# The first sequence's sums of y for layer three: asked for at turns 46 to 52 of layer one, and kept in two tiles

## The chip, the cores and the metric

The kernel runs on one core of a Trainium2 chip, as one launch. The metric is the device time of the launch in microseconds, the median over several executions. One more execution was taken with the hardware profiler; every row below comes from it. Engines are named as in the profile: PE is TensorE (matmuls; PEld its weight loads), DVE is VectorE, ACT is ScalarE, POOL is GpSimd, SP is SyncE, whose queue issues the transfers.

## The reference

Two batch entries ("sequences") of 768 tokens, 512 features; all float32.

```python
x = attention(q, k, v)            # 8 heads of 64; local window and block summaries; 1536 tokens x 512
h = max(x @ w1, x @ w2, x @ w3)   # layer one, 768 wide, a maximum over three products
y = h @ w_out                     # layer two, 512 wide
z = (y @ w_a) * (y @ w_b)         # layer three, 1536 wide, a product of two products
out = z @ w_out2                  # layer four, 512 wide
```

## The kernel before

**Tiles.** The 1536 tokens lie in four chunks of 384, two for each sequence: chunks 0 and 1 are the first sequence, 2 and 3 the second. Features lie on the 128 partitions. Each matrix product is made of three float32r matmuls (high by high, low by high, high by low part), by `mm3` (L511), so an operand is kept as a high part, written by ACT, and a low part, the remainder, written by DVE or POOL (`split`, L514 and L515).

**Layers one and two** (`layers12`) run chunk by chunk. A turn of layer one is 12 matmuls into one PSUM tile `ph` (4 blocks of features, 3 matmuls each); `evac` takes the result out into a tile `t`, by ACT for the first of three (L536) and by DVE, with the maximum, for the other two (L538). The third is split into `hg`, by ACT and POOL. Layer two is four products `py` of 18 matmuls each; ACT copies each into `y` (L564). One chunk has 18 + 4 = 22 turns. The list `TURNS[0]` lays the turns of all chunks out in one order: turns 0 to 43 are chunks 0 and 1, turns 44 to 51 are chunk 2 alone, 52 to 71 alternate between chunks 2 and 3, 72 to 75 are layer two of chunk 2, and 76 to 87 are the rest of chunk 3.

**Layer three** (`layer3`) forms y @ w_a and y @ w_b by a scheme with seven products instead of eight, over both chunks of a sequence and both halves of the features. Its moving operands are seven sums (B11, B21, T1, T2, T3, B22, T4) of quarters of y. `sums_of(c, m)` makes them: the tiles `yd` are differences (DVE, L580); `op` then writes each operand `yt` as a high part (ACT, L575) and a low part (DVE, L576). For the second sequence, `halves` calls it as soon as y is there. For the first sequence y is complete after turn 43, and the main loop calls it at the four turns of `SUMS`: B11, then B21, then T1, then T2, T3, B22 and T4 together. The products go to PSUM tiles `qb`, `qg` and `qd`; ACT and DVE take them out (`s`, `m`, `u` by ACT at L621; `ca` at L631; `t` at L635 and L637).

**Weights.** A weight tile `w` (128x512, 64-bit source) is loaded by SP's queue, put together by ACT (L441, L443), DVE (L445, L446) and POOL (L447), and split into `wt` by ACT (L451) and DVE or POOL (L452). For layer three two such tiles are also combined into sums `s` by DVE (L467 to L470) before the split. Layers three and four alternate over six groups of 256 columns; layer four's products are `po`, added up in `acc`.

**What sets the order.** The program text sets only priorities and dependences. A scheduler, when the kernel is built, puts each engine's instructions into one queue; each engine then works its queue strictly in that order, and an instruction that waits holds up all behind it. `tc.issue_after` adds an order between two instructions on one engine. Layer-three products of the first sequence are put by the scheduler between the `ph` and `py` products of chunks 2 and 3, so part of layer three is done while the layers before it still run.

The lines that call the sums:

```python
GATE, ROOM, SUMS, EARLY34 = (2, 3), 16, (58, 62, 66, 70), 6
...
            with tc.issue_after(mark[0]), tc.issue_after(mark[1]):
                weights(1)
                if i in SUMS:
                    m = SUMS.index(i)
                    sums_of(m // 2, m % 2 * 2 + 1)
```

Of the kernel before, what the change touches and what calls it, by code (L numbers as in the profile page):

```python
# [10 lines left out]
F32R = mybir.dt.float32r  # L11
# [8 lines left out]
P = 128  # L20
# [16 lines left out]
NCH, MAXT = len(CHUNKS), max(SIZES)  # L37
# [21 lines left out]

GATE, ROOM, SUMS, EARLY34 = (2, 3), 16, (58, 62, 66, 70), 6
LEAD, TURN, ERA0, ASKS, AHEAD, PRE, TURNS = 5, (11, 2, 2), 8, (3, 4, 5, 7, 9), (4, 1), 3, ((6, N1 - 6, 6, 4, 4, 8, N1 - 8, 4, 12), (24, 34), (34, 44))


# [11 lines left out]
def attention_then_maxout_then_bilinear(ctx: ExitStack, tc: tile.TileContext, qt, kt, vt, vwin, wall, const, out):  # L77
# [13 lines left out]
    t_p = ctx.enter_context(tc.tile_pool(name="t", bufs=B))  # L91
# [465 lines left out]
        if lastc:  # L557
            w_freed += N2

    ops = {}  # L560

    def halves(c, m, ps):

# [4 lines left out]
    def sums_of(c, m):  # L568

        b, j = divmod(c, 2)  # L570
        (b11, b21), (b12, b22) = ((y[:, 0:2], y[:, 2:4]) for y in (ys[2 * b], ys[2 * b + j]))

        def op(name, src):
            ops[b, name] = t = t_p.tile([P, 2, 2, MAXT * P], F32R, tag=name, name="yt")
            A.activation(t[:, 0], src, AF.Copy)  # L575
            V.tensor_tensor(t[:, 1], src, t[:, 0], ALU.subtract)  # L576

        def diff(tag, x, y):
            t = y_p.tile([P, 2, MAXT * P], F32, tag=tag, name="yd")
            V.tensor_tensor(t, x, y, ALU.subtract)  # L580
            return t

        if j == 0:
            op(("B11", "B21")[m // 2], (b11, b21)[m // 2])
        elif m == 1:
            t1 = sums[b] = diff("t1", b12, b11)
            op("T1", t1)
        else:
            t2 = diff("t2", b22, sums[b])
            op("T2", t2)  # L590
            op("T3", diff("t3", b22, b12))
            op("B22", b22)
            op("T4", diff("t3", b21, t2))
# [201 lines left out]
```

## Time and profile before

| | |
|---|---|
| median of 3 runs | 566.62 us (566.19 to 566.95) |
| the profiled execution | 569.36 us, of which the span from first to last instruction is 567.6 us |
| PE busy | 548.9 us, 97% of the span, 3374 matmuls |
| DVE, ACT, POOL busy | 376.3 us (66%), 278.9 us (49%), 203.0 us (36%) |
| mean granted clock of PE | 0.993 of full speed |

PE is busy nearly all the time, so the kernel's time is the matmuls' time plus the pauses of PE and the stretches in which its clock is lowered. In 40 slices of the span the page shows two where the granted clock is 0.9 (near 250 us and near 310 us); the rest from 14 us on is at full speed.

### The profile page before, as it was taken

Reading aid. Unit: us, or ns where it says so; the run is one execution under the profiler, and the core shown is the slowest. Engines: PE = TensorE matmul, PEld = TensorE weight load, DVE = VectorE, ACT = ScalarE, POOL = GpSimd, SP = SyncE. Lnnn points to the kernel's source line nnn. Section 1 sums busy time; section 2 is a strip of 40 time slices with the busy share of each in tenths; the row PEclk is TensorE's granted clock in tenths of the full one; section 3 lists DMA queues with packets and bytes.
Section 4 is the critical chain, followed back from the end, with each engine's and each line's share of the span. In section 5 each row is a group of like instructions: output and inputs, shape, how many; then the busy total and the mean of one; then the engine's idle time right before and its main releaser. Section 6 shows DMA issues by size and latency. Waiting matters only on the chain.

```text
span 567.6 us, 9050 instructions
## 1 busy us (share of the span) xinstructions
PE 548.9 (97%) x3374; PEld 518.4 (91%) x3374; DVE 376.3 (66%) x781; ACT 278.9 (49%) x667; POOL 203.0 (36%) x177
## 2 busy tenths in 40 slices
PE   7999999999999999999998899999999999999997
PEld 7889999999999999999997899899989989999985
DVE  4798966865432133939969955866868997783374
ACT  4799765666441214534656556445454553341220
POOL 3479996442110111503603413413413242330030
PEclk9999999999999999989999899999999999999999
DMA  8992464843100030212231222122123121000005
GB/s 304 354 270 75 151 233 133 252 145 112 46 1 1 2 111 1 75 38 93 93 112 39 74 70 80 38 74 76 37 75 103 46 76 38 1 0 1 1 29 193
DMA packets 16987, 51.81 MB, mean 91 GB/s; under 512 B 2096, under 2 KB 2480, under 8 KB 16944
## 3 DMA queue, kind: packets, MB, share of 16 engines
q1 hardware_dynamic: 16944, 51.25, 27.6%
q8 instruction: 26, 0.43, 0.3%
q14 instruction: 17, 0.14, 0.1%
HBM read 48.09 MB, written 3.15 MB: 90 GB/s over the span
## 4 chain that ended last, share of the span: by engine, by line
PE 67%; DVE 15%; DMA 7%; ACT 5%; issue 2%; POOL 2%; SPq 1%; ACTq 0%; POOLq 0%; DVEq 0%
PE ph L511 21%; PE qb L511 11%; PE py L511 6%; PE qg L511 5%; PE po L666 4%; PE po L667 4%; PE po L668 4%; DMA w<-wall 4%; DVE wt L452 3%; PE ps L250 3%; PE qd L511 2%; PE psv L305 2%; DVE t L637 2%; DVE w L446 2%; DVE hg L515 2%
## 5 line engine op out<-in xcount | busy, mean ns | idle before, releaser
L511 PE MATMUL ph<-x,wt 128*128 128x384 f32 x864 | 156.3, 337 | 0.0
L511 PEld LDWEIGHTS ph<-x,wt 128*128 128x128 f32 x864 | 149.3, 188 | 0.5 <-DVE x L515 0.3
L447 POOL TENSOR_TENSOR w<-w,w 128x512 int32<-128x512 int32 x60 | 83.2, 1391 | 155.1 <-DVE w L446 96.0
L511 PE MATMUL qb<-yt,wt 128*128 128x384 f32 x576 | 114.6, 339 | 5.5 <-DVE t L637 3.0
L511 PEld LDWEIGHTS qb<-yt,wt 128*128 128x128 f32 x576 | 102.6, 189 | 11.1 <-DVE t L637 3.4
L514 ACT ACTIVATE hg<-t 128x384 fp32r<-128x384 f32 x72 | 36.9, 522 | 86.7 <-DVE t L538 47.9
L638 POOL TENSOR_TENSOR t<-t,ca 128x384 f32<-128x384 f32 x36 | 43.8, 1232 | 85.4 <-DVE t L637 85.3
L511 PE MATMUL qg<-yt,wt 128*128 128x384 f32 x288 | 60.0, 345 | 2.0 <-DVE t L637 1.0
L678 DVE TENSOR_TENSOR acc<-po,acc 128x512 f32<-128x512 f32 x60 | 40.8, 686 | 27.1 <-PE po L668 27.1
L538 DVE TENSOR_TENSOR t<-ph,t 128x384 f32<-128x384 f32 x48 | 26.5, 552 | 45.8 <-PE ph L511 44.7
L666 PE MATMUL po<-wt,hg 128*128 128x512 f32 x144 | 56.3, 391 | 0.6 <-ACT hg L514 0.6
L667 PE MATMUL po<-wt,hg 128*128 128x512 f32 x144 | 56.6, 393 | 0.0
L511 PEld LDWEIGHTS qg<-yt,wt 128*128 128x128 f32 x288 | 52.4, 194 | 4.5 <-DVE t L637 1.7
L668 PE MATMUL po<-wt,hg 128*128 128x512 f32 x144 | 56.1, 395 | 0.1
L511 PE MATMUL py<-hg,wt 128*128 128x384 f32 x288 | 56.0, 343 | 0.1
L511 PEld LDWEIGHTS py<-hg,wt 128*128 128x128 f32 x288 | 50.2, 190 | 0.5 <-ACT y L564 0.4
L257 ACT ACTIVATE s<-s,nm 128x120 f32<-128x120 f32 x96 | 37.1, 390 | 23.2 <-DVE nm L256 22.6
L515 POOL TENSOR_TENSOR hg<-t,hg 128x384 fp32r<-128x384 f32 x24 | 27.1, 1134 | 50.5 <-ACT hg L514 49.3
L451 ACT ACTIVATE wt<-w 128x512 fp32r<-128x512 f32 (+1 forms) x60 | 35.1, 586 | 18.6 <-PE qb L511 14.4
L515 DVE TENSOR_TENSOR hg<-t,hg 128x384 fp32r<-128x384 f32 x48 | 40.6, 855 | 3.9 <-ACT hg L514 3.9
L452 DVE TENSOR_TENSOR wt<-w,wt 128x512 fp32r<-128x512 f32 (+1 forms) x44 | 30.5, 694 | 14.4 <-ACT wt L451 14.4
L443 ACT ACTIVATE w<-w 128x512 int32<-128x512 uint32 x60 | 39.2, 667 | 0.6 <-DMA w<-wall 0.6
(80 smaller groups left out, 779.9 us busy)
## 6 DMA issues: line engine op xcount, KB each, us to landing
w<-wall SPq DMA_DIRECT2D x60, 512.0 KB, 3.5
q<-qt SPq DMA_DIRECT2D x15, 384.0 KB, 6.9
row<-kt SPq DMA_DIRECT2D x8, 416.0 KB, 5.0
full<-vt SPq DMA_DIRECT2D x8, 384.0 KB, 7.2
out<-acc SPq DMA_DIRECT2D x12, 256.0 KB, 2.0
v<-vwin SPq DMA_DIRECT2D x12, 192.0 KB, 5.4
v<-vwin SPq DMA_DIRECT2D x12, 96.0 KB, 5.6
q<-qt SPq DMA_DIRECT2D x1, 256.0 KB, 4.1
```

What stands on the lines that cost most here:

```text
L257: A.activation(s[:, a], s[:, a], AF.Exp, bias=nm[:, a:a + 1], scale=-1.0, accum_out=sm[:, a:a + 1])
L443: A.activation(lw.bitcast(I32), lw, AF.Copy, scale=2.0 ** -29)
L447: G.tensor_tensor(w.bitcast(I32), w.bitcast(I32), lw.bitcast(I32), ALU.add)
L452: eng.tensor_tensor(w[:, 1], r, w[:, 0], ALU.subtract)
L511: T.matmul(ps, w[:, i, o:o + P], x[:, j], start=first and n == 0, stop=last and n == 2, skip_group_check=more)
L514: A.activation(dst[:, 0], src, AF.Copy)
L515: eng.tensor_tensor(dst[:, 1], src, dst[:, 0], ALU.subtract)
L638: G.tensor_tensor(t, t, cs[c, f], ALU.mult)
L666: T.matmul(ps, g[:, 0], w[:, 0], start=(f == 0), stop=False)
L667: T.matmul(ps, g[:, 0], w[:, 1], start=False, stop=False)
L668: T.matmul(ps, g[:, 1], w[:, 0], start=False, stop=(f == 1))
L678: V.tensor_tensor(acc[c, i], ps, acc[c, i], ALU.add)
```

## The change

The four turns at which the first sequence's sums are called move from 58, 62, 66 and 70 to 46, 48, 50 and 52. The operands of the first sequence lie in two tiles, one for B11 and B21 and one for T1, T2, T3, B22 and T4, where each had a tile of its own; the second sequence keeps seven tiles.

```diff
-GATE, ROOM, SUMS, EARLY34 = (2, 3), 16, (58, 62, 66, 70), 6
+GATE, ROOM, SUMS, EARLY34 = (2, 3), 16, (46, 48, 50, 52), 6
...
-    ops = {}
+    ops, both = {}, {}
...
         def op(name, src):
-            ops[b, name] = t = t_p.tile([P, 2, 2, MAXT * P], F32R, tag=name, name="yt")
+            names = next(x for x in (("B11", "B21"), ("T1", "T2", "T3", "B22", "T4")) if name in x) if b == 0 else (name,)
+            if name == names[0]:
+                both[b, names] = t_p.tile([P, len(names), 2, 2, MAXT * P], F32R, tag=names[0] + str(b), name="yt", bufs=1)
+            ops[b, name] = t = both[b, names][:, names.index(name)]
             A.activation(t[:, 0], src, AF.Copy)
             V.tensor_tensor(t[:, 1], src, t[:, 0], ALU.subtract)
```

Instructions and their sizes are the same in both kernels; their order differs on every engine's queue. Line numbers behind the new lines are three higher (L576 is L579, L580 is L583). With the two tiles alone, and the old turns, every queue has the order of before.

On DVE, from the first maximum of layer one of chunk 2 on (`t<-ph` are maxima, `yd` and `yt` the sums), the queue before was:

```order
L538 TENSOR_TENSOR t_2333<-ph,t_2318 128x384
L538 TENSOR_TENSOR t_2349<-ph,t_2333 128x384
L538 TENSOR_TENSOR t_2381<-ph,t_2366 128x384
L538 TENSOR_TENSOR t_2397<-ph,t_2381 128x384
L538 TENSOR_TENSOR t_2429<-ph,t_2414 128x384
L538 TENSOR_TENSOR t_2445<-ph,t_2429 128x384
L538 TENSOR_TENSOR t_2493<-ph,t_2463 128x384
L538 TENSOR_TENSOR t_2508<-ph,t_2478 128x384
L538 TENSOR_TENSOR t_2523<-ph,t_2493 128x384
L576 TENSOR_TENSOR yt<-y,yt 128x768
L538 TENSOR_TENSOR t_2544<-ph,t_2508 128x384
L538 TENSOR_TENSOR t_2592<-ph,t_2562 128x384
```

and is now:

```order
L538 TENSOR_TENSOR t_2333<-ph,t_2318 128x384
L579 TENSOR_TENSOR yt<-y,yt 128x768
L538 TENSOR_TENSOR t_2352<-ph,t_2333 128x384
L579 TENSOR_TENSOR yt<-y,yt 128x768
L538 TENSOR_TENSOR t_2386<-ph,t_2369 128x384
L538 TENSOR_TENSOR t_2402<-ph,t_2386 128x384
L583 TENSOR_TENSOR yd<-y 128x768
L579 TENSOR_TENSOR yt<-yd,yt 128x768
L538 TENSOR_TENSOR t_2439<-ph,t_2424 128x384
L583 TENSOR_TENSOR yd<-y,yd 128x768
L583 TENSOR_TENSOR yd<-y 128x768
L579 TENSOR_TENSOR yt<-y,yt 128x768
```

Nearly all sums of the first sequence stand now between the maxima of chunk 2's first eight turns; before, the first of them stood behind nine maxima.

On DVE, where the first three weight tiles of layer three are worked on (`w`, `s`, `wt`) and the last maxima of chunk 2 are taken, the queue before was:

```order
L580 TENSOR_TENSOR yd<-y,yd 128x768
L580 TENSOR_TENSOR yd<-y 128x768
L576 TENSOR_TENSOR yt<-y,yt 128x768
L538 TENSOR_TENSOR t_2785<-ph,t_2711 128x384
L452 TENSOR_TENSOR wt<-w_2722,wt 128x512
L467 TENSOR_TENSOR s<-w_2729 128x256
L469 TENSOR_TENSOR s<-w_2722,w_2729 128x256
L576 TENSOR_TENSOR yt<-yd,yt 128x768 x2
L445 TENSOR_SCALAR w_2897<-psw 128x512
L468 TENSOR_TENSOR s<-s,w_2722 128x256
L452 TENSOR_TENSOR wt<-w_2729,wt 128x256
L580 TENSOR_TENSOR yd<-y,yd 128x768
```

and is now:

```order
L538 TENSOR_TENSOR t_2780<-ph,t_2724 128x384
L452 TENSOR_TENSOR wt<-w_2735,wt 128x512
L467 TENSOR_TENSOR s<-w_2742 128x256
L469 TENSOR_TENSOR s<-w_2735,w_2742 128x256
L468 TENSOR_TENSOR s<-s,w_2735 128x256
L470 TENSOR_TENSOR s<-w_2735,s 128x256
L445 TENSOR_SCALAR w_2892<-psw 128x512
L446 SCALAR_TENSOR_TENSOR w_2892<-psw,w_2892 128x512
L452 TENSOR_TENSOR wt<-w_2742,wt 128x256
L452 TENSOR_TENSOR wt<-s,wt 128x512 x2
L579 TENSOR_TENSOR yt<-y,yt 128x768 x2
```

The sums `yd` and `yt` of the first sequence are gone from between the steps of the weights; the two `yt` at the end are the second sequence's.

On PE, from the end of the last `ph` product before layer two of chunk 2 on, the queue before was:

```order
L511 MATMUL qb<-yt,wt 128x384
L511 MATMUL qd<-yt,wt 128x384
L511 MATMUL py<-hg,wt 128x384 x30
L511 MATMUL qb<-yt,wt 128x384 x5
L511 MATMUL py<-hg,wt 128x384 x4
L511 MATMUL qd<-yt,wt 128x384 x2
L511 MATMUL py<-hg,wt 128x384 x2
L511 MATMUL qd<-yt,wt 128x384 x3
L511 MATMUL qg<-yt,wt 128x384
L511 MATMUL qb<-yt,wt 128x384
L511 MATMUL qg<-yt,wt 128x384 x5
L511 MATMUL qb<-yt,wt 128x384 x5
```

and is now:

```order
L511 MATMUL py<-hg,wt 128x384 x17
L511 MATMUL qb<-yt,wt 128x384 x6
L511 MATMUL py<-hg,wt 128x384 x19
L511 MATMUL qg<-yt,wt 128x384 x6
L511 MATMUL qb<-yt,wt 128x384 x4
L511 MATMUL py<-hg,wt 128x384 x36
L511 MATMUL qb<-yt,wt 128x384 x2
L511 MATMUL qd<-yt,wt 128x384 x3
L511 MATMUL ph<-x,wt 128x384 x12
```

The first layer-three product comes later, behind 17 matmuls of layer two, and six matmuls of it stand together; 25 matmuls stand now between `qb`'s first six and its next four, where 12 stood. From the second sequence's sums on, the queues of all engines have the same order in both kernels, but for a few neighbours on PE (`qg`, `qb`, `po`) and one `yt` on ACT.

## Rows read from the trace of the kernel before

**Rows 1.** Busy time by stretch: PE, PEld, DVE, ACT, POOL, then granted clock, DMA.
```profile
180.00:200.00 20.00, 20.00 (x117) 20.00 (x116) 2.98 (x6) 4.28 (x8) 3.03 (x3) 1.00 0.00 1
...
240.00:260.00 20.00, 18.36 (x95) 17.86 (x94) 10.44 (x17) 6.95 (x13) 3.20 (x3) 0.91 0.08 27
...
280.00:300.00 20.00, 19.14 (x107) 18.17 (x106) 14.53 (x19) 12.29 (x23) 4.21 (x4) 1.00 0.32 103
300.00:320.00 20.00, 16.95 (x88) 16.40 (x87) 19.73 (x30) 10.45 (x22) 10.68 (x8) 0.91 0.13 44
```

**Rows 2.** The same view in stretches of 2 us around both pauses.
```profile
242.00:244.00 2.00, 1.67 (x6) 1.67 (x7) 2.00 (x4) 1.61 (x3) 0.00 (x0) 0.66 0.64 184
244.00:246.00 2.00, 2.00 (x8) 2.00 (x7) 1.08 (x2) 0.80 (x2) 0.00 (x0) 0.50 0.19 78
...
314.00:316.00 2.00, 2.00 (x9) 1.98 (x8) 2.00 (x3) 0.83 (x2) 2.00 (x3) 0.58 0.00 0
316.00:318.00 2.00, 2.00 (x8) 2.00 (x8) 2.00 (x2) 1.01 (x2) 2.00 (x3) 0.56 0.00 0
```

**Rows 3.** Chain that ended last: start, length (us), what; layer-one products without a pause.
```profile
175.24 50.19 PE ph L511 x288
```

**Rows 4.** PE in order of time: start, length (us), tile; idle before and releaser.
```profile
231.50 0.34 PE L511 MATMUL qb<-yt,wt 128*128 128x384 f32 x1
...
240.95 0.44 PE L511 MATMUL qb<-yt,wt 128*128 128x384 f32 x1 [0.71 <-ACT s L621]
242.33 1.72 PE L511 MATMUL qg<-yt,wt 128*128 128x384 f32 x5 [0.94 <-DVE wt L452]
...
255.00 0.34 PE L511 MATMUL qb<-yt,wt 128*128 128x384 f32 x1
...
285.41 6.83 PE L511 MATMUL py<-hg,wt 128*128 128x384 f32 x36
292.07 1.57 PE L511 MATMUL qg<-yt,wt 128*128 128x384 f32 x8
...
299.63 3.41 PE L511 MATMUL qb<-yt,wt 128*128 128x384 f32 x18 [0.73 <-ACT u L621]
...
313.56 1.68 PE L511 MATMUL qb<-yt,wt 128*128 128x384 f32 x6 [3.05 <-DVE t L637]
```

**Rows 5.** DVE in order of time, layer one and the stretch before the first pause.
```profile
210.93 0.56 DVE L538 TENSOR_TENSOR t<-ph,t 128x384 f32<-128x384 f32 x1 [5.70 <-PE ph L511]
...
228.85 1.27 DVE L580 TENSOR_TENSOR yd<-y,yd 128x768 f32<-128x768 f32 x1
230.04 2.06 DVE L580 TENSOR_TENSOR yd<-y 128x768 f32<-128x768 f32 x1
232.03 1.77 DVE L576 TENSOR_TENSOR yt<-y,yt 128x768 fp32r<-128x768 f32 x1
233.73 0.54 DVE L538 TENSOR_TENSOR t<-ph,t 128x384 f32<-128x384 f32 x1
...
235.46 1.81 DVE L576 TENSOR_TENSOR yt<-yd,yt 128x768 fp32r<-128x768 f32 x2
...
238.69 0.95 DVE L580 TENSOR_TENSOR yd<-y,yd 128x768 f32<-128x768 f32 x1
...
240.50 1.78 DVE L452 TENSOR_TENSOR wt<-s,wt 128x512 fp32r<-128x512 f32 x1
```

**Rows 6.** POOL in order of time, the first two weight tiles of layer three.
```profile
228.00 3.29 POOL L447 TENSOR_TENSOR w<-w,w 128x512 int32<-128x512 int32 x2 [8.53 <-issue]
```

**Rows 7.** ACT in order of time, evacuations of the last layer-two products.
```profile
288.31 0.47 ACT L564 ACTIVATE y<-py 128x384 f32<-128x384 f32 x1
...
291.84 0.93 ACT L564 ACTIVATE y<-py 128x384 f32<-128x384 f32 x2
```

**Rows 8.** DVE in order of time, second sequence's sums to second pause.
```profile
292.85 0.95 DVE L580 TENSOR_TENSOR yd<-y,yd 128x768 f32<-128x768 f32 x1
...
312.96 0.54 DVE L637 TENSOR_TENSOR t<-qb,m 128x384 f32<-128x384 f32 x1
```

**Rows 9.** What SP's queue of transfers waited for, 195 to 330 us: total, times, longest.
```profile
SPq L421 <- POOL w L447: 99.4, 12, 18.8
```

## The prediction

> **What bounds the kernel now.** I read the page's busy shares first: PE works 97% of the span at a mean clock of 0.993, so a change that leaves the matmuls alone can gain only what PE loses in pauses and in lowered clock. The forty slices of the page put the lowered clock at two places, and the table of stretches is the view that narrows them down: in the 20 us from 240 and from 300 the granted clock is 0.91, and beside them it is 1.00 [rows 1]. In stretches of 2 us it is 0.66 and 0.50 right behind the first pause, and 0.58 and 0.56 right behind the second [rows 2]; these four account for both 0.91 ((0.34 + 0.50) x 2 / 20 = 0.084, and 0.086), so elsewhere in those 40 us the clock is full. 0.50 is the lower of the clock's two levels, 1.2 GHz against 2.4; the others are mixtures of the two. PE in order of time then shows what each pause waits for [rows 4]: at 240.95 for an ACT copy `s` (0.71 us), at 242.33 for the low part of a weight sum, a `wt` by DVE (0.94), at 299.63 for ACT's `u` (0.73), at 313.56 for DVE's `t` (3.05).
>
> The change rewrites what DVE does ahead of the first pause, so DVE in order of time is the view to stay with [rows 5]. From 228.85 to 242.28 it has no pause; the `wt` that PE waits for ends at 242.28, and PE starts at 242.33. Between 228.85 and that end stand six sums of the first sequence. The rows give `yd` 1.27, `yd` 2.06, `yt` 1.77, two `yt` in 1.81 and `yd` 0.95: 7.86 by durations, about 7.5 from start to next start, since neighbours overlap by some 0.08. So more than half of DVE's 13.4 us there is work that the pause does not need.
>
> **The change, part by part.** It removes no instruction and adds none; it moves them, and the rest is order.
>
> *The sums' new place.* On DVE they go among the first maxima of chunk 2. There DVE is busy 2.98 of 20 us, ACT 4.28 and POOL 3.03 [rows 1], and later it once waits 5.70 us for a product [rows 5]. The eleven steps (four `yd`, seven `yt`) at 0.95 us (the undisturbed row at 238.69) are 10.5 us of DVE work, for which about 17 idle us in every 20 are there. What is queued behind a sum is the next maximum, and behind that the PSUM tile that PE wants again. One product takes 12 x 50.19/288 = 2.09 us [rows 3], of which a maximum uses 0.56 [rows 5], so three sums in a row (0.95 + 0.95 + 0.90 = 2.80) make the next maximum late by 2.80 - 1.53 = 1.27 us. Does PE feel 1.27? The trace of before has such a case: the maximum at 233.73 to 234.27 takes out a product that ended 12 layer-two matmuls (2.09 us) ahead of 231.50, at about 229.4. It came out 4.9 us late, and PE's rows show no wait for it. I cost the new place at nothing, with 4.9 us as cover.
>
> *The first pause (A).* With the sums gone, DVE's chain to the late `wt` is 13.4 - 7.5 = 5.9 us of other rows. What starts that chain is POOL's last step on the first two weight tiles, which ends at 228.00 + 3.29 = 231.29 [rows 6]; 231.3 + 5.9 = 237.2. PE now asks later: 43 matmuls stand between the first product of layer three's old place (231.50 [rows 4]) and the first matmul that needs this `wt` (17 `py`, 6 `qb`, 19 `py` and one), so at 231.5 + 43 x 0.1743 = 239.0. The margin is 1.8 us. The other wait, 0.71 for ACT's `s`, had 12 matmuls (2.1 us) between the product and its reuse, and has 25 (4.4 us) now: 2.1 + 0.71 = 2.8 was needed, 4.4 is there. Both waits should go, and with them the lowered clock. PE from 231.50 to 255.00 [rows 4] spent 23.50 us on 113 matmuls; at 0.1743 each they take 19.70. **A = 3.80 us** (0.71 + 0.94 of waits, 2 x 0.34 + 2 x 0.50 = 1.68 of clock, and 0.47 of smaller gaps). The bounds are 0 (a new wait of the same length) and 3.80.
>
> On that lowered clock, first the rows: at 240.95 to 242.33 PE idled for 1.65 us in two pieces, and 0.66 and 0.50 followed [rows 2, 4]; behind the single pause of 0.73 at 299.63 the clock stayed full, by the account above. The Trainium skill (TensorE: Matmul & The Clock Gate, What's actually happening) says that the gate is set by how busy the engine has recently been, and that the throttled state is the default which activity lifts. Here that agrees with both rows. By it the whole 1.68 comes back with the pauses; were the lowered clock tied to the place in the program and not to idling, the gain would be 3.80 - 1.68 = 2.12.
>
> *The end of layer two (B).* In the last 36 `py` matmuls, 285.41 to 292.07, PE takes 6.66 us for 6.27 of work [rows 4]. Two rows say why: ACT's copy of a `py` tile comes only at 288.31 [rows 7], ACT being held until then behind a weight step that waits for its data. The new order has PE there about 4 us earlier while the weight steps also come earlier, and PE's queue has three other matmul groups ahead of it. **B = 0.39**; bounds 0 and 0.39, or less than nothing if the weight's transfer keeps its old time (a rival, below).
>
> *Start of the second sequence's sums (C).* PE ends the last `py` at 292.07, ACT does two copies in a row from 291.84 (0.93 us) and DVE starts the first `yd` at 292.85, 0.78 later [rows 7, 8]. A single copy takes 0.47, so with the copy of the tile before done in time this is about 0.5: **C = 0.25**; bounds 0 and 0.3.
>
> *The second pause.* From 292.85 to 313.50 DVE works through the second sequence's sums and the weights of the next products, 19.73 busy of the 20 us from 300 [rows 1, 8], and the `t` at the end releases PE at 313.56. This chain is in the same order after, so it keeps its 20.7 us, its start moves with PE, and the waits of 0.73 and 3.05 and the lowered clock behind them stay. Gain 0 here; what was gained ahead is carried through, neither more nor less.
>
> *Transfers.* SP's queue waits, in 195 to 330, 12 times and 99.4 us in all for POOL's `w` step, which frees a weight buffer [rows 9]. So the transfers are paced by the engines, come earlier by what the engines come earlier, and cost nothing; if they were not, the price is in the third rival.
>
> Sum: 3.80 + 0.39 + 0.25 = 4.44 us. The profiled execution's own time is 569.36, so 564.92 by its measure. It lies 2.74 above the median of 566.62; I take the same loss off the median: **562.2**. The forecast's own range is 561.2 to 563.2 (the clock's share moves with where a pause falls; B and C may be nothing).
>
> **The rivals.**
> *Part of the pause stays* (0.10). The wait of 0.71 for `s` is a matter of PSUM tiles and not of DVE. If ACT is again late there, PE idles 0.71, maybe with the lowered clock: 562.2 + 0.71 = 562.9, or with 1.68 of clock 564.6. Against it speak the 25 matmuls of cover. The Trainium skill (Perfetto Trace Analysis, Optimization Strategy) reads a recurring gap as a possible lack of room for the next tile; the 0.71 here, named for ACT's copy out, agrees with that reading, and by it the gap would stay.
>
> *The second pause shrinks too* (0.08). If DVE's freed time lets weight steps run ahead of the second sequence's sums, up to 3.05 of wait and 2 x 0.42 + 2 x 0.44 = 1.72 of clock come back: 562.2 - 4.77 = 557.4, with half of it 559.8. Against it: the queues from there on are in the old order, and a strict order lets nothing slip ahead.
>
> *The gain is given back at the second pause* (0.06). If the weights there come at a fixed time, not with the engines, PE waits 3.05 + 4.44 = 7.5 us there: 566.6, no change. Against it speaks that the queue of transfers waits for POOL [rows 9].
>
> *Slower, by new waits in layer one* (0.06). If the PSUM tiles of layer one are only two deep, a maximum late by 1.27 stops PE. At the three places where sums stand two or three in a row that is 3.8 us, and with the lowered clock behind two of them (1.7 each) 7.2: 562.2 + 7.2 = 569.4. It decides from 4.4 us of such waits. The row of 233.73 speaks against it. It grows if the sums are stretched: the `yd` at 230.04 took 2.06, not 0.95, while POOL worked [rows 5, 6]. The Trainium skill (GPSIMD Engine Reference, Key points) says that GpSimd shares its SBUF interfaces with VectorE and contends with VectorE instructions that read two SBUF inputs, as these do; the stretched row agrees. POOL is busy only 3.03 of 20 us at the new place [rows 1], so few sums should meet it.
>
> **How the numbers follow.** The forecast has 0.70, the rivals 0.10, 0.08, 0.06 and 0.06. A measurement of this kernel tells about 0.2%, 1.13 us, from no change, so faster is below 565.5: the forecast, the first and the second rival, 0.88; same 0.06; slower 0.06. The range is 560.5 to 564.9: it leaves out most of the second rival, the third and the fourth, and holds the first.
>
> **What would show it.** In the changed kernel's profile the stretch of 240 to 260 has a granted clock of 1.00 and 20 us of PE work; `yd` and `yt` of the first sequence lie at about 177 to 205 among the maxima, and PE has no wait there. The first `qb` of layer three is at about 234.5; the last `py` ends near 287.7; a pause of some 3 us for DVE's `t` ends near 309, with a clock of about 0.57 behind it, and from there on all is as before, 4.4 us earlier. The prediction is wrong if PE waits for `t` or for ACT between 175 and 232, if the `wt` of the weight sum is still late at 239, or if the second pause is over 1 us longer or shorter than 3.05.

## The result and the profile after

The changed kernel takes 561.87 us (561.15 to 562.06, four executions) against 566.79 for the kernel before: the medians lie 4.9 us or 0.9% apart, and the ratio of the runs is 0.9891 (95% interval 0.9862 to 0.9919), so the change is faster by about 1%. In a later comparison it took 562.34 against 567.05, ratio 0.9922 (0.9892 to 0.9952).

The table of stretches of the changed kernel (time; then busy time of PE, PEld, DVE, ACT, POOL; granted clock; share of DMA):

```profile
180.00:200.00 20.00, 20.00 (x117) 20.00 (x117) 12.85 (x16) 7.00 (x11) 2.20 (x2) 1.00 0.00 1
...
240.00:260.00 20.00, 20.00 (x117) 20.00 (x116) 12.43 (x20) 7.70 (x15) 3.91 (x3) 1.00 0.15 53
...
300.00:320.00 20.00, 15.90 (x85) 14.29 (x84) 18.35 (x27) 12.79 (x26) 9.81 (x8) 1.00 0.23 79
```

Against [rows 1], DVE's work in 180 to 200 grew from 2.98 to 12.85 us and PE stayed at 20.00; 240 to 260 is full, at full clock; 300 to 320 still has its pause. PE in order of time (start, length, tile; in brackets idle time before and who ended it):

```profile
232.00 1.20 PE L511 MATMUL qb<-yt,wt 128*128 128x384 f32 x6
...
236.34 1.20 PE L511 MATMUL qg<-yt,wt 128*128 128x384 f32 x6
237.38 0.85 PE L511 MATMUL qb<-yt,wt 128*128 128x384 f32 x4
...
278.98 6.40 PE L511 MATMUL py<-hg,wt 128*128 128x384 f32 x36
285.22 2.24 PE L511 MATMUL qg<-yt,wt 128*128 128x384 f32 x12
...
292.56 3.42 PE L511 MATMUL qb<-yt,wt 128*128 128x384 f32 x18 [0.58 <-ACT u L624]
...
306.20 1.33 PE L511 MATMUL qb<-yt,wt 128*128 128x384 f32 x6 [2.95 <-DVE t L640]
...
312.94 2.35 PE L511 MATMUL qb<-yt,wt 128*128 128x384 f32 x12 [0.95 <-DVE t L638]
```

The chain that ended last has the run of layer one as one piece, with its start ahead of the first moved sum:

```profile
172.86 56.36 PE ph L511 x324
```

That last row is needed to read the others. The two profiled executions already differ by 175.24 - 172.86 = 2.38 us where that run begins [rows 3], before any queue of the two kernels differs. Freed of these 2.38, the end of the last `py` is 292.07 - 285.22 - 2.38 = 4.47 us earlier, the wait for `u` ends 299.63 - 292.56 - 2.38 = 4.69 earlier, the second pause ends 313.56 - 306.20 - 2.38 = 4.98 earlier, and the span is 567.6 - 559.3 - 2.38 = 5.9 us shorter [rows 4]. The last 0.9 come from behind the second pause, where this execution kept its full clock (1.00 in 300 to 320), while before lost 1.7 there [rows 2]; part of that was handed back as the wait of 0.95 at 312.94, since DVE is the bound there.

DVE in order of time, among layer one's maxima and then at the first weight steps of layer three:

```profile
175.18 0.56 DVE L538 TENSOR_TENSOR t<-ph,t 128x384 f32<-128x384 f32 x1 [0.94 <-PE ph L511]
...
191.27 2.64 DVE L579 TENSOR_TENSOR yt<-yd,yt 128x768 fp32r<-128x768 f32 x2
193.83 0.95 DVE L583 TENSOR_TENSOR yd<-y,yd 128x768 f32<-128x768 f32 x1
195.69 0.96 DVE L579 TENSOR_TENSOR yt<-yd,yt 128x768 fp32r<-128x768 f32 x1 [0.91 <-ACT yt L578]
196.57 0.55 DVE L538 TENSOR_TENSOR t<-ph,t 128x384 f32<-128x384 f32 x1
...
233.39 2.41 DVE L452 TENSOR_TENSOR wt<-s,wt 128x512 fp32r<-128x512 f32 x2
...
285.94 0.96 DVE L583 TENSOR_TENSOR yd<-y,yd 128x768 f32<-128x768 f32 x1 [0.67 <-ACT y L564]
```

The two late `wt` are there at 234.08 (the first, of 0.69 us) and at 235.80 (the second). PE comes for the first with the `qg` at 236.34, 2.3 us later, and for the second later still: no wait. The maximum at 196.57 is late: counted from the one at 175.18, which PE released, nine products of 2.09 us later is 193.97, so it waited 2.6 us in the queue, and PE did not notice.

### The profile page after: what moved, and what is told of

Same layout as the page of the kernel before. It is cut to its first block, busy times and chain, and to the rows that moved or that the text cites. A ratio compares the mean times of both kernels' runs of the same rounds, so it can differ in the third digit from the quotient of the medians.

```text
span 559.3 us, 9056 instructions
## 1 busy us (share of the span) xinstructions
PE 543.4 (97%) x3374; PEld 513.6 (92%) x3374; DVE 376.6 (67%) x781; ACT 278.0 (50%) x667; POOL 200.8 (36%) x177
## 4 chain that ended last, share of the span: by engine, by line
PE 77%; DVE 12%; DMA 4%; ACT 3%; issue 2%; POOL 2%; SPq 0%; POOLq 0%; DVEq 0%; ACTq 0%
PE ph L511 24%; PE qb L511 13%; PE py L511 9%; PE qg L511 5%; PE po L671 5%; PE po L670 5%; PE po L669 5%; PE qd L511 3%; PE ps L250 3%; DVE wt L452 2%; DVE hg L515 2%; DMA w<-wall 2%; PE psv L305 2%; PE pst L286 1%; DVE t L640 1%
## 5 line engine op out<-in xcount | busy, mean ns | idle before, releaser
L511 PE MATMUL qb<-yt,wt 128*128 128x384 f32 x576 | 112.9, 336 | 5.5 <-DVE t L640 2.9
L511 PE MATMUL qg<-yt,wt 128*128 128x384 f32 x288 | 58.0, 336 | 0.5 <-DVE t L640 0.5
L511 PEld LDWEIGHTS qg<-yt,wt 128*128 128x128 f32 x288 | 50.6, 188 | 2.8 <-DVE t L640 1.0
L452 DVE TENSOR_TENSOR wt<-w,wt 128x512 fp32r<-128x512 f32 (+1 forms) x44 | 32.4, 737 | 16.2 <-ACT wt L451 16.2
```

The source lines that it names most:

```text
L452: eng.tensor_tensor(w[:, 1], r, w[:, 0], ALU.subtract)
L511: T.matmul(ps, w[:, i, o:o + P], x[:, j], start=first and n == 0, stop=last and n == 2, skip_group_check=more)
```

## The experiments

Each execution is known with its mean granted clock, and each profile with the start of the last transposition of the attention (tile `pst`), which lies ahead of everything that the change moves. The table takes that start off the profiled execution's own time; what is left ("rest") can be compared between kernels without the early part.

```
kernel                  median   ratio to before (95%)     own time  pst     rest
before                                                     569.36    170.07  399.29
changed                 561.87   0.9891 (0.9862-0.9919)    561.15    167.72  393.43
after_again             562.34   0.9922 (0.9892-0.9952)    562.34    168.52  393.82
tiles_only              565.45   0.9961 (0.9945-0.9976)    566.69    168.03  398.66
other_place             566.44   0.9987 (0.9968-1.0006)    565.31    168.22  397.09
four_inside             565.85   0.9978 (0.9958-0.9997)    568.04    169.96  398.08
first_two_late          562.11   0.9909 (0.9889-0.9930)    561.82    168.10  393.72
one_yt_inside           563.82   0.9936 (0.9915-0.9957)    563.67    170.09  393.58
low_part_4x             563.22   0.9929 (0.9907-0.9952)    563.24    169.40  393.84
load_known              562.50   0.9918 (0.9889-0.9947)    563.27    168.55  394.72
pool_two                563.74   0.9938 (0.9920-0.9955)    563.77    168.82  394.95
products_on_dve_all     561.88   0.9905 (0.9881-0.9928)    562.28    167.94  394.34
products_on_dve_first   568.31   1.0022 (1.0001-1.0043)    570.64    169.90  400.74
products_on_dve_third   564.74   0.9967 (0.9951-0.9984)    563.70    168.30  395.40
```

**The changed kernel once more: after_again.** No edit.

> The changed kernel once more, as it is, beside the next three on one chip. Theory: 561.9 +- 0.6; the profile again shows no PE wait between 225 and 260, and the pause of 2.9 to 3.0 for DVE's t near 306; whether the clock is lowered behind it may differ between executions. Rival (the first profile without a lowered clock behind the second pause is what the change does): clock full behind 306 again.

562.34, no wait between 225 and 260, the second pause 2.93, and this time with the clock lowered behind it (its rows stand further below).

**The tiles without the turns: tiles_only and other_place.**

```diff
-GATE, ROOM, SUMS, EARLY34 = (2, 3), 16, (46, 48, 50, 52), 6
+GATE, ROOM, SUMS, EARLY34 = (2, 3), 16, (58, 62, 66, 70), 6
```

> Two tiles for the first sequence's sums, turns 58, 62, 66 and 70 as before; every queue has the order of before. Theory (the gain is DVE's time between the first weight steps of layer three): 566.6 +- 0.6, ratio 1.000, both pauses there, PE waiting about 0.9 for a wt near 242 and about 3 for t near 313. Rival (the layout itself gives part of the gain): 565.5 or less. On the clock: if the lowered clock follows the pauses in every execution, each execution shows a mean granted clock near 0.993; if it comes and goes, some show 0.997 or more at nearly the same time less 1.7 to 3.4 us.

And with that the five last operands in one tile, B11 and B21 apart:

```diff
-names = next(x for x in (("B11", "B21"), ("T1", "T2", "T3", "B22", "T4")) if name in x) ...
+names = next(x for x in (("B11",), ("B21",), ("T1", "T2", "T3", "B22", "T4")) if name in x) ...
```

> Old turns; B11 and B21 in tiles of their own, the last five operands in one: every queue has the order of before, and the tiles lie at a third set of SBUF addresses (before and the two-tile kernel with old turns have two others). If the 1.2 to 2.2 us between before and the two-tile kernel with old turns belong to the place in memory: this one may lie anywhere in 564.5 to 568, and its early part (up to 170) differs from both by its own waits for x or s. If any merging gives it: 565.4 +- 0.5. If it is chance between executions: the median lies between the two, 565.4 to 567.6, and its executions spread over 3 us or more.

PE's waits in both, tiles_only first:

```profile
238.89 0.44 PE L511 MATMUL qb<-yt,wt 128*128 128x384 f32 x1 [0.78 <-ACT s L624]
240.27 1.14 PE L511 MATMUL qg<-yt,wt 128*128 128x384 f32 x5 [0.93 <-DVE wt L452]
...
311.47 1.33 PE L511 MATMUL qb<-yt,wt 128*128 128x384 f32 x6 [3.23 <-DVE t L640]
```

```profile
239.10 0.44 PE L511 MATMUL qb<-yt,wt 128*128 128x384 f32 x1 [0.80 <-ACT s L624]
240.48 1.16 PE L511 MATMUL qg<-yt,wt 128*128 128x384 f32 x5 [0.94 <-DVE wt L452]
...
309.96 1.40 PE L511 MATMUL qb<-yt,wt 128*128 128x384 f32 x6 [2.99 <-DVE t L640]
```

Both pauses are those of before, to within 0.2 us: the tiles alone remove nothing. What differs is the clock behind the first pause. Stretches of 2 us, tiles_only and then other_place:

```profile
242.00:244.00 2.00, 2.00 (x8) 2.00 (x7) 1.11 (x2) 1.06 (x3) 0.00 (x0) 0.50 0.16 66
```

```profile
242.00:244.00 2.00, 2.00 (x13) 2.00 (x13) 1.32 (x2) 1.17 (x3) 0.00 (x0) 1.00 0.30 121
```

After the same two waits at the first pause PE did 8 matmuls in 2 us in one execution and 13 in the other. So the lowered clock follows the pause in some executions and not in others, and a fixed 1.68 us for it is too much: the rests of the two kernels, 398.66 and 397.09, lie 1.6 apart. The four executions of tiles_only with a mean clock of 1.000 took 564.8 to 565.5, the three at 0.994 took 566.2 to 566.7.

tiles_only is 0.4% faster than before with the same queues. That was not expected: 565.45 lies at the bound of the rival by which the layout gives part of the gain. other_place, at a third set of addresses, can't be told from before. The executions of before in these comparisons run from 564.5 to 571.7 us, and of the 2.7 us between the profiled executions of before and tiles_only, 2.0 lie ahead of the mark (170.07 against 168.03), where the change does nothing. Whether the place in memory or chance made tiles_only's 0.4% stays open. Against tiles_only, first_two_late (below, with the same tiles) gained 3.3 us in the same comparison; against other_place the changed kernel gained 4.1. By the medians that is what the turns bring: 3.3 to 4.1 us.

The traces say it more sharply. From the mark to the end of the last `py` before the second sequence's sums, the kernels with the new order on PE take the same time to within 0.1 us, and those with the old order take longer:

```
before 122.00   tiles_only 121.73   other_place 120.42
changed 117.50   after_again 117.49   first_two_late 117.50   one_yt_inside 117.58
low_part_4x 117.50   pool_two 117.50
```

So up to there the turns take away 4.2 to 4.5 us where the clock fell behind the first pause (before, tiles_only) and 2.9 us where it stayed full (other_place).

**Which sums, and how far: first_two_late, one_yt_inside, four_inside.**

```diff
-GATE, ROOM, SUMS, EARLY34 = (2, 3), 16, (46, 48, 50, 52), 6
+GATE, ROOM, SUMS, EARLY34 = (2, 3), 16, (58, 62, 50, 52), 6    first_two_late
+GATE, ROOM, SUMS, EARLY34 = (2, 3), 16, (58, 62, 64, 66), 6    one_yt_inside
+GATE, ROOM, SUMS, EARLY34 = (2, 3), 16, (58, 62, 66, 68), 6    four_inside
```

> Turns 58, 62, 50 and 52: B11 and B21 stay at their old turns, T1 and the last four operands are made early. PE's queue is that of the changed kernel. Theory: the two yt of B11 and B21 lie in DVE's idle time at either place, so the time is that of the changed kernel, 561.9 +- 0.6, and no PE wait near 235 to 245. Rival (all four must move): 563 to 565.

> Turns 58, 62, 64 and 66: the sums are made only a little earlier than before, and one yt (0.9 us) still stands on DVE between the first weight steps; PE's queue is that of the changed kernel. Theory: wt is ready at 237.2 + 0.9 = 238.1 against 239.0 needed (in the times of the kernel before), so no wait: 561.9 to 562.3. Rival (the sums must be out of the whole stretch, or early for its own sake): 563 or more.

> Turns 58, 62, 66 and 68: four steps of the sums (three yt, one yd, 3.55 us) still stand on DVE between the first weight steps, where six stood; PE has an order of its own, in which the wt of the sum is needed 49 matmuls after the first product of layer three's old place (240.0). Theory: wt ready at 237.2 + 3.55 = 240.8, a wait of 0.8, with or without 1.7 of lowered clock: 562.7 to 564.5. Rival (only the last position counts): 566.6 as before.

first_two_late is the changed kernel again (562.11, rest 393.72): B11 and B21 need not move. one_yt_inside has the same rest, 393.58, and no wait near 240, so the sums need not be early, only out of the way of the weights; its median is 1.5 us over what was expected and in the range of its rival, but its profile has that time in the early part, as a wait that no other profile has at this size:

```profile
68.40 6.88 PE L511 MATMUL ph<-x,wt 128*128 128x384 f32 x38 [1.45 <-DVE x L515]
```

All four of its executions lie between 563.1 and 564.1, so this may belong to its place in memory; that was not tried. four_inside (565.85, expected 562.7 to 564.5) missed its range. By its ratio it is 0.2% below before, but against tiles_only, which has the same tiles and ran beside it (565.45), it gained nothing. Its waits:

```profile
239.49 1.15 PE L511 MATMUL qb<-yt,wt 128*128 128x384 f32 x5 [1.36 <-DVE wt L452]
...
287.25 3.42 PE L511 MATMUL py<-hg,wt 128*128 128x384 f32 x18 [1.01 <-ACT y L564]
```

The wait of 1.36 is where it was expected and longer by 0.6 (it is for the first weight's low part, not for the sum's), and the wait for ACT's `y`, which is term B of the prediction, is there at 1.01. From the mark to the end of the last `py` it takes 120.54 us, at full clock behind its pause, which is other_place's 120.42. So the place of the wait is as the theory says, and the price of what was left inside is not: with four of the six sums there, nothing was won. The time does not speak against the rival (only the last position counts); only the rows do, which show other waits than before. How the gain grows with the number of sums moved is not shown.

**Load that the order knows of: load_known.**

```diff
-            V.tensor_tensor(s12[:, 0:256], a21, a22, ALU.add)
+            for _ in range(21 if n == 0 and kind == 'a' else 1):
+                V.tensor_tensor(s12[:, 0:256], a21, a22, ALU.add)
```

> The changed kernel in which DVE works out the first weight sum of layer three 21 times instead of once (the same result), 6.8 us more between the first weight steps, nearly what the sums of y took there before; the queues were laid out with these steps in view, so PE's order is another: the first product that needs the late wt stands 102 matmuls after layer three's old place, not 43. Theory A (a pause comes where PE's order asks for a wt earlier than DVE has it): wt ready at 237.2 + 6.8 + 0.9 (one yt stands there too) = 244.9 against 231.5 + 102 x 0.1743 = 249.3 needed, in the times of the kernel before; no wait, 562 to 563. Theory B (so much DVE work between the weight steps costs its time whatever the order): pause of 1.5 or more near 240, 564.5 to 566.5.

DVE's late `wt` and PE's products that need it:

```profile
245.46 1.29 DVE L452 TENSOR_TENSOR wt<-s,wt 128x512 fp32r<-128x512 f32 x2 [0.24 <-ACT wt L451]
```

```profile
247.39 0.33 PE L512 MATMUL qg<-yt,wt 128*128 128x384 f32 x1
...
247.91 1.03 PE L512 MATMUL qg<-yt,wt 128*128 128x384 f32 x5
```

Both `wt` are ready only at 246.75, 11 us later than in the changed kernel (10 counted from the mark), and PE has no wait, because its products stand behind 59 more matmuls, 36 of them of layer two and 12 of layer one. The time is 562.50, as expected by theory A: DVE's load between the weight steps costs nothing by itself. The second wait of the first pause was PE's order asking at 241.4 for what DVE's order gave at 242.28. No run has the new order on PE with the old queue on DVE; it would ask 43 matmuls behind layer three's old place, where the old order asked behind 50, so by the rows PE's new order alone would not have removed that wait.

**The price in layer one: low_part_4x.**

```diff
             V.tensor_tensor(t[:, 1], src, t[:, 0], ALU.subtract)
+            for _ in range(3 * (b == 0)):
+                V.tensor_tensor(t[:, 1], src, t[:, 0], ALU.subtract)
```

> The changed kernel in which DVE works out each low part of the first sequence's sums four times over (the same result, 21 steps more, some 18 us of DVE work in layer one of chunk 2); PE's queue is unchanged. By the order of DVE's queue the maxima of layer one come up to 5.3 us late. Theory (the cover for late maxima is at least 4.9 us): no PE wait, or under 0.5, in 175 to 215; 561.9 to 562.6. Rival (two PSUM tiles, cover 2.1 us): PE stops for 3 us or more there, and with lowered clock the time is 565 to 568.

DVE in order of time, and the table of stretches:

```profile
176.86 0.56 DVE L538 TENSOR_TENSOR t<-ph,t 128x384 f32<-128x384 f32 x1 [0.93 <-PE ph L511]
...
201.58 0.54 DVE L538 TENSOR_TENSOR t<-ph,t 128x384 f32<-128x384 f32 x1
```

```profile
190.00:200.00 10.00, 10.00 (x59) 10.00 (x59) 10.00 (x12) 3.21 (x5) 1.11 (x1) 1.00 0.01 2
200.00:210.00 10.00, 10.00 (x60) 10.00 (x59) 9.96 (x13) 1.06 (x3) 1.74 (x2) 1.00 0.00 0
```

DVE is full for 20 us; the maximum at 201.58 was due nine products after 176.86, at 195.65, and is 5.9 us late. PE is busy without a gap, and from the mark to the end of the last `py` it takes 117.50 us, the changed kernel's time. The slower rival, which needed PE to stop when a maximum is 1.3 us late, is out by a factor of more than four. (The median is 0.6 over the expected range; in the profile the mark lies at 169.40, 0.9 later than in after_again, which ran beside it.)

**The second pause: pool_two, and the products on DVE.** The changed kernel leaves a pause of 2.9 us; these four tried to win it. First, two low parts of the second sequence's sums on POOL:

```diff
-            V.tensor_tensor(t[:, 1], src, t[:, 0], ALU.subtract)
+            (G if b == 1 and name in ('B22', 'T4') else V).tensor_tensor(t[:, 1], src, t[:, 0], ALU.subtract)
```

> The changed kernel with two low parts of the second sequence's sums (B22 and T4) on POOL instead of DVE; PE, ACT and SP keep their queues and all tiles their place. Theory (the second pause is DVE's chain of 20.7 us, which the first change left alone): the chain gets 1.75 shorter (two steps of 0.87), less up to 1 of stretching by POOL beside two-input steps; PE's wait for t of 2.95 shrinks to 1.2 to 2.0 and the time to 560.2 to 561.2. Rival (the weights set that pause, by their transfers): the wait stays near 2.9 and the time at 561.9.

POOL, DVE and PE in order of time:

```profile
288.03 2.56 POOL L579 TENSOR_TENSOR yt<-y,yt 128x768 fp32r<-128x768 f32 x1 [7.98 <-ACT yt L578]
```

```profile
289.04 3.23 DVE L579 TENSOR_TENSOR yt<-yd,yt 128x768 fp32r<-128x768 f32 x2 [0.16 <-ACT yt L578]
...
294.94 1.54 DVE L452 TENSOR_TENSOR wt<-w,wt 128x512 fp32r<-128x512 f32 x1 [1.81 <-ACT wt L451]
```

```profile
294.44 2.37 PE L511 MATMUL qb<-yt,wt 128*128 128x384 f32 x12 [1.36 <-ACT u L624]
...
308.64 1.55 PE L511 MATMUL qb<-yt,wt 128*128 128x384 f32 x6 [3.02 <-DVE t L640]
```

Slower than the changed kernel by 1.4 us. DVE lost two steps of 0.87, but the two `yt` beside POOL's step took 3.23 instead of 1.82 and the `wt` beside its second took 1.54 instead of 0.69; ahead of that `wt` DVE stood 1.81 for ACT, which had been held behind the late last `yd`. Nothing was won from the chain. The expectation allowed 1 us of stretching; it was 2.3, and a new wait.

Then the reverse: layer three's last product (`t` times `ca`) from POOL to DVE, for all six groups of columns, for the first group alone, and for one quarter of z (a third of these steps).

```diff
-                        G.tensor_tensor(t, t, cs[c, f], ALU.mult)
+                        V.tensor_tensor(t, t, cs[c, f], ALU.mult)                        products_on_dve_all
+                        (V if n == 0 else G).tensor_tensor(t, t, cs[c, f], ALU.mult)     products_on_dve_first
+                        (V if j == 0 else G).tensor_tensor(t, t, cs[c, f], ALU.mult)     products_on_dve_third
```

> The changed kernel with layer three's last product (t times ca, 36 steps of 1.2 us on POOL) on DVE. Theory (the second pause is DVE's chain, and POOL's two-input steps stretch it: s at 1.23 for 0.41 beside POOL's t): the chain loses some 2 us of stretching ahead of 306 and gains two steps of 0.47, so the pause shrinks by about 1 and the time to 560.8 to 561.9, unless DVE's 17 us more elsewhere make new waits. Rival (DVE is the bound after 290, more work there is later work): 563 or more.

> The same only for the first of the six groups of columns, where the second pause lies. Theory: the pause of 2.9 shrinks by about 1, the rest as the changed kernel, 560.8 to 561.8. Rival (more work on DVE in its busiest stretch): 562.5 or more.

> The changed kernel with a third of the last products of layer three on DVE (those of one quarter of z: 12 of 36 steps); PE's queue is that of the changed kernel up to the fourth group of columns. Theory (POOL's two-input step beside DVE's s steps stretches them): one of the two POOL steps at 300 to 303 goes, so one of the two s steps falls from 1.23 to 0.41, DVE gains one step of 0.47, and the pause shrinks by 0.35 to 0.5, from 2.93 to about 2.5, with no new wait of ACT near 318: 561.3 to 562.2. Rival (the new wait for ACT's s near 318 comes with any such move): 562.3 or more.

The changed kernel's steps on DVE and POOL, and then those of products_on_dve_all on DVE and PE:

```profile
300.74 1.23 DVE L467 TENSOR_TENSOR s<-w 128x256 f32<-128x256 f32 x1
301.90 1.23 DVE L469 TENSOR_TENSOR s<-w,w 128x256 f32<-128x256 f32 x1
...
300.23 2.62 POOL L641 TENSOR_TENSOR t<-t,ca 128x384 f32<-128x384 f32 x2
```

```profile
301.83 0.55 DVE L641 TENSOR_TENSOR t<-t,ca 128x384 f32<-128x384 f32 x1
302.30 0.41 DVE L467 TENSOR_TENSOR s<-w 128x256 f32<-128x256 f32 x1
302.63 0.55 DVE L641 TENSOR_TENSOR t<-t,ca 128x384 f32<-128x384 f32 x1
303.10 0.41 DVE L469 TENSOR_TENSOR s<-w,w 128x256 f32<-128x256 f32 x1
...
306.25 1.33 PE L511 MATMUL qb<-yt,wt 128*128 128x384 f32 x6 [1.89 <-DVE t L640]
...
318.24 3.76 PE L511 MATMUL qb<-yt,wt 128*128 128x384 f32 x12 [1.81 <-ACT s L624]
```

The same `s` steps fall from 1.23 to 0.41 us when POOL is not at its product, so DVE does four steps in the time of two and PE's pause is 1.89 instead of 2.9: the stretching is shown, and the pause shrinks by the size expected (1). But the gain returns 12 us later as a wait of 1.81 for ACT's `s`, under an order that the move also changed, and the time is the changed kernel's (561.88). products_on_dve_first shows the same 1.90 at the pause and then 7.5 us of waits behind 320, where the changed kernel has 2.1, and in 315 to 335 its granted clock is 0.91 where the changed kernel's is 1.00. These 5.4 and 1.8 us are nearly all of the 7.3 by which its rest is longer; why its order makes those waits was not followed up. In products_on_dve_third the one POOL step that is left stretches DVE's own product to 1.38: its pause is 2.73 (expected 2.5), the time 564.74, with 1.2 us more of waits behind 320 and without the wait near 318 that its rival named. Both were expected near 561 to 562 and are slower. No version tried is clearly faster than the changed kernel.

## Why the prediction was right

The forecast of 562.2 came within 0.4 us of the first measurement and 0.2 of the second. The place of the gain and its mechanism hold. That the number fits so closely is in part luck: a clock loss that does not come in every execution was counted in full, and a difference of before to the kernels with its own queues, which the sum did not have, went the other way.

**The sums' new place at nothing: right.** PE has no wait between 175 and 292 in the changed kernel. The lateness of a maximum was put at 1.27 and is 2.6: four sums stand in a row from 191.27 to 196.57, two of them took 2.64 instead of 1.82 beside a POOL step, and one waited 0.91 for ACT. The cover was put at 4.9 from one row that shows less. The maximum at 233.73 starts 4.3 us behind its product's end (4.9 is to its own end), the 12 matmuls behind that product are layer one's, and then PE turns to layer three and layer two, so the row does not say when layer one would have wanted the tile. low_part_4x is what shows the cover, at least 5.9.

**A = 3.80, of which 1.68 clock: waits right, clock too firm.** Both waits are gone: layer three begins at 232.00 + 2.38 = 234.4 in the times of before (forecast 234.5), and the late `wt` is ready 2.3 us before PE asks (forecast 1.8). For the wait of 0.71 the prediction named the wrong owner. It called it "a matter of PSUM tiles and not of DVE" and relied on 25 matmuls of cover. ACT's queue, before and then after, shows DVE behind it too:

```profile
239.67 0.85 ACT L575 ACTIVATE yt<-yd 128x768 fp32r<-128x768 f32 x1 [0.57 <-DVE yd L580]
240.42 0.47 ACT L621 ACTIVATE s<-qb 128x384 f32<-128x384 f32 x1
```

```profile
233.24 0.49 ACT L624 ACTIVATE s<-qb 128x384 f32<-128x384 f32 x1
```

Before, the product for `s` ended at 238.16, and `s` stood behind a copy of a sum that waited for DVE. Now the product ends at 233.20 and `s` starts at once, so the cover was not needed. The profiled execution of before, on which the sum was made, had lost the clock at both pauses; other_place shows the same pause without that loss. The term is 2.12 of waits and small gaps, and 0 to 1.7 of clock. With B and C as measured that makes 2.6 to 4.3, against 4.44 forecast, and the turns brought 3.3 to 4.1 by the medians. Between before and the kernels with its own queues the medians of their comparisons differ by another 0.6 to 2.2 us, which was not in the sum, and so the measured difference is 4.9.

**B = 0.39: right.** The last 36 `py` take 285.22 - 278.98 = 6.24 us instead of 6.66, 0.42 less. A and B together were to be 4.19 at the end of the last `py`, and are 4.47 against the profile of before, which had lost the clock.

**C = 0.25: too large.** The first `yd` starts 0.72 us behind the last `py` (285.94 - 285.22) where it was 0.78: 0.06. ACT's single copy and its release take nearly what the two took.

**The second pause stays: right.** 2.95 after 3.05, ended at 306.20 + 2.38 = 308.6 (forecast: near 309). DVE's chain ahead of it, which was to keep its 20.65 us (292.85 to 313.50), took 20.21, from the first `yd` at 285.94 to the end of the `t` that releases PE at 306.15. With these 0.44, which the prediction put at nothing, 4.47 + 0.06 + 0.44 = 4.97 us make up the 4.98 by which the pause ends earlier. The lowered clock behind it was forecast too, and it is missing in the first profile and there in the second (after_again, stretches of 2 us):

```profile
306.00:308.00 2.00, 1.04 (x3) 1.04 (x4) 2.00 (x4) 0.30 (x1) 1.01 (x2) 0.65 0.00 0
308.00:310.00 2.00, 2.00 (x7) 2.00 (x7) 2.00 (x4) 1.36 (x3) 2.00 (x2) 0.50 0.00 0
```

**The rivals.** Part of the pause stays: no, both waits went. The second pause shrinks too: no, by 0.1 alone. The gain given back at the second pause: no. Slower by layer one: no, by low_part_4x. That DVE's steps were stretched by POOL [rows 5, 6] was used only for that last rival; the runs on the second pause show that it matters more. There a two-input step of 128x256 beside POOL takes three times as long (0.41 to 1.23). The Trainium skill (GPSIMD Engine Reference, Key points) names this contention, and these rows agree with it. It may also be why the first pause was there at all: the stretched sums and the last `wt` cost 3.0 us over their undisturbed times (2.06 + 1.77 + 1.78 - 0.95 - 0.95 - 0.68) in rows 5, and PE waited 1.65. That is argued from the rows and was not tried.

## What to carry to other kernels

When PE waits for a step of another engine, list what stands ahead of that step in that engine's queue and ask which of it the step does not need; such work can go wherever that engine idles, provided that the work it delays there has a cover that the trace already shows. Load on an engine need be no cost in itself (load_known); a cost comes where the waiting engine's order asks too early for the result. Before moving a step to an idle POOL, look at what DVE does at the same time: the move may stretch DVE's steps by more than it takes off.

## What the runs showed of the hardware

The lowered clock behind a pause is not fixed to the pause: after two waits of 0.8 and 0.9 us PE ran at 0.50 in one execution and at 1.00 in another of a kernel with the same queues, and after a pause of 2.9 us both were seen in two executions of one kernel. Where DVE is the bound behind the pause, the full clock is not all gain: the changed kernel's first profile, without the loss, has a wait of 0.95 for DVE instead.

Two-input DVE steps of 128x256 took 0.41 us alone and 1.23 beside a POOL product; two of 128x768 took 1.82 alone and 3.23 beside a POOL subtraction. In the kernel before a step with one input was stretched as well, from 0.41 to 1.42, beside a POOL step of 1.38:

```profile
301.94 0.41 DVE L445 TENSOR_SCALAR w<-w 128x512 uint32<-128x512 uint32 x1
...
304.04 1.42 DVE L445 TENSOR_SCALAR w<-w 128x512 uint32<-128x512 uint32 x1
```

```profile
303.79 1.38 POOL L447 TENSOR_TENSOR w<-w,w 128x512 int32<-128x512 int32 x1 [17.27 <-DVE w L446]
```

The early part, in which none of these edits changes the order of a queue, reaches the transposition named above at 167.7 to 170.1 us. That spread, 2.4 us, is half of the change's effect, so a profile's own time should be read from a common mark onward: from there to the end of layer two the kernels with the same order on PE agreed to within 0.1 us.
